# Mask factors in a room of the mixing from the first batch on, GpSimd for a pair's last sums, and another order of the last outputs, in a fused BigBird attention and Fourier mixing kernel

## The chip, the cores and the metric

The kernel runs on one core of a Trainium2 chip. A core has a matrix engine (TensorE, PE in the profile), VectorE (DVE), ScalarE (ACT), GpSimd (POOL), SyncE (SP), which here issues nearly all transfers, and 16 DMA engines that carry them. The metric is the device time of one execution in microseconds; the times shown are those of several runs, and the profile is that of one execution.

## The reference

Four batches of eight heads, 768 tokens, head width 64. Block-sparse attention with blocks of 32 tokens is followed by a Fourier mixing and a two-layer channel network on the 512 features of each token:

```python
scores = scale * q @ k.T
mask = near_diagonal | first_or_last_block | sampled_blocks      # by blocks of 32
attn = softmax(where(mask, scores, -1e9))
x = (attn @ v) laid out as (batch, token, head * width)

mixed = real(fft(fft(x, axis=1), axis=2))
u = x + mixed
un = (u - mean(u)) / sqrt(var(u) + 1e-6)
out = u + relu(un @ w_ch1) @ w_ch2          # w_ch1: 512 x 2048, w_ch2: 2048 x 512
```

The channel weights arrive as 64-bit floats, so they come as 16 MB and are rounded to 32 bits on the core.

## The kernel before

**Attention.** Two heads are a pair; there are 16 pairs, four to a batch. A pair has two halves of the queries (384 each) and six chunks of 128 keys, so 12 *units* (half, chunk), each a 128 x 768 tile of scores for both heads. Two units are a *slot*, 24 slots a batch. `scores` makes the score tiles on PE (line 570), `weigh` takes the exponent on ACT, `values` multiplies by v on PE (line 633) one slot later.

**The mask** is applied in two ways. In the first batch, and in the second until the channel network of batch 0 starts, PE adds a product of two small bf16 factors to the scores (`scores`, line 580), which puts blocked positions at a large negative value; such units are in `by_pe`, and ACT's exponent writes the weights directly (line 590). Later a 0/1 mask multiplies the exponents on DVE (lines 593 and 595). The factors are `of_k` and `off_q`; a third array, `keep_q`, serves to make the 0/1 mask. In the kernel before they lie in the two buffers of the pool `acc_p` (`at_k`, `at_q`). At slot 19 (`SB - 5`) `keep_factors` has GpSimd copy `of_k` and `off_q` to the large buffer `big2`, so that the `acc_p` buffers become free for batch 1.

**Row sums.** In batch 0 PE sums each unit's weights (`add_up`, line 701). From batch 1 on `gather` adds a half's six units up in a tile `acc` (pool `acc_p`, two buffers), either on DVE (line 614, one instruction of 128x768) or on GpSimd (line 619, two of 128x384), and `total` takes the sum over the partitions of both halves' `acc` on PE (line 715). For units in `by_pe`, `gather` is called in `values`, right after a unit's products, and picks the engine by the planner's clock; for the others it is called in `weigh`, and always GpSimd. The weights `e` have four buffers: the exponent of slot k+2 needs those of slot k released, by `values` and by `gather`.

**The channel weights.** 32 chunks of 512 KB come into large buffers `big0` to `big5` ("rooms", six of them, in turn: `w_load`), and `w_round` rounds each with two ACT instructions (lines 450, 453) and five on DVE (454 to 462), 1.42 chunks a slot. A chunk's load can go when the chunk six before it is rounded. `slot` emits the loads (`w_loads`) and then the rounding (`w_steps`). All loads stand in one queue on SP, in the order in which they are emitted: weights, q, k and v of coming pairs, and the cosine tables; one that must wait holds those behind it.

**The mixing** of batch b runs on PE, DVE and ACT between the slots of batch b+1, and that of the last batch after all attention. It folds x (`fold_0` to `fold_2`, DVE), multiplies by cosine and sine tables (`along`, `across`), normalizes (`spread`, `whiten`), transposes (`un_flip`), and then runs the channel network (`quad`, line 1032; `channels`, line 1088). The last batch uses `outputs` (line 1151), a form of block multiplication with seven products for each of three row tiles, twice; the results are added to the rows xA and xB on DVE (line 1158), and `store` sends finished rows out (line 1099).

**The order of the work** is written out by hand: instructions are emitted in program order for each engine. A planner keeps an estimated clock of each engine (`when`, advanced by `busy`), and places steps of the mixing (`gap`, `do_apart`) and short steps by those clocks; it also chooses DVE or GpSimd in `gather`. It runs when the program is built, not on the chip.

Of the kernel before, what the change touches and what calls it, by code (L numbers as in the profile page):

```python
# [11 lines left out]
FP32 = mybir.dt.float32  # L12
# [70 lines left out]
def _rows(view, tile):  # L83

    got = []
    for t, p0, runs, jump, n, s0, step in _ORDER:
        if t != tile:
            continue
        at = view[s0:s0 + 1, :]
        row, col = list(at.ap[0])[0], list(at.ap[1])  # L90
        if jump > 0:
            got.append((p0, runs * n, bass.AP(tensor=at.tensor, offset=at.offset,
                                              ap=[[jump * row, runs], [step * row, n], col])))
            continue
        for r in range(runs):
            at = view[s0 + r * jump:s0 + r * jump + 1, :]
            got.append((p0 + r * n, n, bass.AP(tensor=at.tensor, offset=at.offset,
                                               ap=[[step * row, n], col])))
    return got
# [3 lines left out]
def kernel(  # L103
# [14 lines left out]
    nc = tc.nc  # L118
# [73 lines left out]
    def busy(engine, us, after=0.0):  # L192
        when[engine] = max(when[engine], after) + us
        return when[engine]
# [10 lines left out]

    HOP = 0.1

    pairs = [(b, j) for b in range(B) for j in range(NP)]
    loaded, v_of = {}, {}

# [113 lines left out]
                                pattern=pat)  # L324


    at_k = acc_p.tile([P, 2, 2 * HS], BF16, tag="acc", name="at_k")
    at_q = acc_p.tile([P, 2, 2 * HS], BF16, tag="acc", name="at_q")
    of_k, off_q, keep_q = at_k[:, 0, :], at_q[:, 0, :], at_q[:, 1, :]

    nc.vector.memset(of_k, 0.0)
    nc.vector.memset(off_q, 0.0)
# [99 lines left out]
                              ap=[[2 * cols, P], [1, 2 * WN]])  # L432
                wchunks.append((src, w_sb[:, row, col:col + WN]))
    wraw = {}
    ROOMS = 6
    def room(i, shape, name, dtype=FP32):
        return big.tile(shape, dtype, tag=f"big{i}", name=name)

    def w_load(i):
        t = room(i % ROOMS, [P, 3 * WN], "wraw", U32)  # L440
        nc.sync.dma_start(out=t[:, 0:2 * WN].bitcast(I32), in_=wchunks[i][0])
        wraw[i] = t

# [25 lines left out]

    by_pe = set()
    factors = {"at": (of_k, off_q)}

    def keep_factors():

        kept = room(2, [P, 2, S], "factors", BF16)
        for a, t in enumerate(factors["at"]):
            nc.gpsimd.tensor_copy(out=kept[:, a, :], in_=t)
        factors["at"] = kept[:, 0, :], kept[:, 1, :]  # L480

    turned, e_of, acc_of, o_of, sums_of, x_of, sp_of = {}, {}, {}, {}, {}, {}, {}
    s_at, e_at, e_free, oT_at, acc_at = {}, {}, {}, {}, {}
# [69 lines left out]
    def scores(us):  # L553

        n, w = divmod(us[0], UP)
        half = w // C
        qT, kT = turned[n, 0], turned[n, 1]
        queries = slice(half * HS, (half + 1) * HS)
        got = []
        for u in us:  # L560
            c = u % C
            s = ps_s.tile([P, 2, 512], FP32, tag="s", name="s")
            got.append((u, s))
            if n < NP or (factors["at"] and True):
                by_pe.add(u)
            busy("PE", 0.72, max(e_at.get(u - SLOT, 0.0), z_at[u % 2]))
            s_at[u] = when["PE"] + HOP
            for i in range(2):
                rows = slice(D * i, D * i + D)
                nc.tensor.matmul(s[:, i, 0:HS], kT[rows, c * P:(c + 1) * P], qT[rows, queries],  # L570
                                 start=True, stop=u not in by_pe)
        for u, s in got:
            if u not in by_pe:
                continue
            c, (at_k, at_q) = u % C, factors["at"]
            busy("PE", 0.25)
            s_at[u] = when["PE"] + HOP
            for i in range(2):
                rows = slice(D * i, D * i + D)
                nc.tensor.matmul(s[:, i, 0:HS], at_k[rows, c * P:(c + 1) * P], at_q[rows, queries],  # L580
                                 start=False, stop=True)
        return got

    def weigh(u, s):
        n, w = divmod(u, UP)
        half, c = divmod(w, C)
        e = ep.tile([P, 2, HS], FP32, tag="e", name="e")
        e_of[u] = e
        if u in by_pe:
            nc.scalar.activation(out=e, in_=s[:, :, 0:HS], func=ACT.Exp, scale=scale)  # L590
            e_at[u] = busy("ACT", 0.8, max(s_at[u], e_free.pop(u - 2 * SLOT, 0.0))) + HOP
        else:
            nc.scalar.activation(out=s[:, :, 0:HS], in_=s[:, :, 0:HS], func=ACT.Exp, scale=scale)  # L593
            m = mask[:, c, half * HS:(half + 1) * HS].rearrange("p (o s) -> p o s", o=1)
            nc.vector.tensor_tensor(out=e, in0=s[:, :, 0:HS], in1=m.broadcast_to([P, 2, HS]),  # L595
                                    op=ALU.mult)
            e_at[u] = busy("DVE", 0.97, busy("ACT", 0.8, s_at[u]) + HOP) + HOP
            if n >= NP:
                gather(u)

    def gather(u):


        n, w = divmod(u, UP)
        half, c = divmod(w, C)
        if c == 0:
            return
        if c == 1:
            acc_of[n, half] = acc_p.tile([P, 2, HS], FP32, tag="acc", name="acc")
        acc, e = acc_of[n, half], e_of[u]  # L610
        start = e_of[u - 1] if c == 1 else acc
        at = max(e_at[u], acc_at.get((n, half), 0.0))
        if u in by_pe and factors["at"] and max(when["DVE"], at) + 1.0 < max(when["POOL"], at) + 2.9:
            nc.vector.tensor_tensor(out=acc, in0=start, in1=e, op=ALU.add)
            acc_at[n, half] = busy("DVE", 1.0, at) + HOP
        else:

            for i in range(2):
                nc.gpsimd.tensor_add(out=acc[:, i, :], in0=start[:, i, :], in1=e[:, i, :])  # L619
            acc_at[n, half] = busy("POOL", 2.9, at) + HOP  # L620
        e_free[u] = acc_at[n, half]

    def values(u):
        n, w = divmod(u, UP)
        half, c = divmod(w, C)
        e = e_of[u]
        busy("PE", 0.75, e_at[u])
        vt = v_of[n]
        if c == 0:
            o_of[n, half] = ps_o.tile([P, HS], FP32, tag="o", name="o")  # L630
        o = o_of[n, half]
        for i in range(2):
            nc.tensor.matmul(o[D * i:D * i + D, :], vt[:, i, c, :], e[:, i, :],  # L633
                             start=(c == 0), stop=(c == C - 1))
        if u in by_pe and n >= NP:
            gather(u)
        if c == C - 1:
            if half == 1:
                v_of.pop(n)
            oT = sum_p.tile([P, HS], FP32, tag="oT", name="oT")  # L640
            if in_blocks(n):
                nc.vector.transpose(out=oT, in_=o_of.pop((n, half)))
                oT_at[n, half] = busy("DVE", 0.5, when["PE"] + HOP) + HOP
            else:
                nc.scalar.copy(out=oT, in_=o_of.pop((n, half)))
                oT_at[n, half] = busy("ACT", 0.5, when["PE"] + HOP) + HOP
            o_of[n, half] = oT
# [295 lines left out]
    def mixer(b, xA, xB):  # L943
# [149 lines left out]
            if r == NF // 4 - 1:  # L1093
                store(half, m)

        def store(half, m):
            x = (xA, xB)[half]
            for p0, cnt, rows in _rows(out[b], T * half + m):
                nc.sync.dma_start(out=rows, in_=x[p0:p0 + cnt, m, :])
            if m == T - 1:  # L1100
                finished.add((b, half))

# [34 lines left out]
        def outputs(r, m, after):  # L1137
# [43 lines left out]
               in1=u.rearrange("p (o d) -> p o d", o=1).broadcast_to([P, 2, DH]), op=ALU.add)  # L1181
            busy("DVE", 0.7)
            plus(b1, p5)
            ahead(2)
            plus(b0, product(ps_s, "s", a22, rights[4]))
            if r == 1:
                store(1, m)
            ahead(3)
            p3 = product(ps_m, "m", o_s[m, 4], block(r, 1, 1))
            plus(a1, p3)  # L1190
            if r == 1:
                store(0, m)
            ahead(4)

        fl = [[("tm"[h == 1 and m != 1], lambda h=h, m=m: un_flip(h, m), 0.6, 0.55, 0.0)
               for m in range(T)]
# [105 lines left out]
    def begin(b):  # L1302


        before, after, rest = mixer(b, x_of[b, 0], x_of[b, 1])
        any_of = len(late) + len(apart) + 4 * len(rest)
        hold = 2 * T
        apart.extend((*step, any_of) for step in norm_steps(b) + before)
        apart.extend((*step, hold) for step in after)

        def go():
            late.extend(rest)
            factors["at"] = None
        apart.append(("-", go, 0.0, 0.0, 0.0, hold))

    def rest():
# [7 lines left out]
        return True  # L1324

    def w_loads():
        while state["got"] < min(len(wchunks), state["w"] + ROOMS):
            w_load(state["got"])
            state["got"] += 1

# [5 lines left out]
    def slot(sl):  # L1336
# [114 lines left out]
            item[2]()  # L1451
        w_loads()
        w_steps(sl)
        if sl == SB - 5:
            keep_factors()
        if sl >= 4 and sl % 2 == 0:
            table_step()

# [139 lines left out]
```

## Time and profile before

| | |
|---|---|
| median of 3 runs | 1077.72 us (1076.29 to 1078.42) |
| profiled execution | 1078.02 us, its span 1075.9 us |
| PE | 1042.7 us busy, 97% of the span |
| DVE | 665.4 us, 62% |
| ACT | 375.7 us, 35% |
| GpSimd | 231.1 us, 21% |
| mean granted PE clock | 0.991 |
| moved by DMA | 46.65 MB |

The span runs from the first to the last instruction of the core; the profiled execution takes 2.1 us more around it. Busy time is what the profile records for each engine; matmuls are pipelined, so busy is not the same as running at the peak. The granted clock is the share of full speed that PE was given. In the profile, lines with an L are lines of the kernel before, and a wait is put down to the engine and line that released it.

### The profile page before, as it was taken

How to read it: one execution, taken by the hardware profiler on the slowest of the kernel's cores; microseconds unless marked ns; L12 is line 12 of the kernel's file. 1: busy time of each engine (PE TensorE's matmuls, PEld its weight loads, DVE VectorE, ACT ScalarE, POOL GpSimd, SP SyncE). 2: the span in 40 equal slices, each digit the busy share in tenths (PEclk: the TensorE clock that was granted, in tenths of full speed). 3: DMA queues.
4: the chain of work that ended last, by engine and by line, in shares of the span. 5: the costliest groups of instructions: out<-in, count | busy, mean ns of one | idle time of the engine just before them, and what ended most of it. 6: DMA issues, size and time to landing. Idle time of an engine off the chain costs nothing.

```text
span 1075.9 us, 12388 instructions
## 1 busy us (share of the span) xinstructions
PE 1042.7 (97%) x4378; PEld 536.5 (50%) x4378; DVE 665.4 (62%) x1226; ACT 375.7 (35%) x742; POOL 231.1 (21%) x258
## 2 busy tenths in 40 slices
PE   8999898999999999999999999999999999999996
PEld 4433344444355555444444555443444555568575
DVE  5899694776771644664568446565556364675663
ACT  5998664563411202353352202243330302210210
POOL 1000080332700001256455001354630001000000
PEclk9999898999999999999999999999999999999998
DMA  7757230220100001222211000221000001000001
GB/s 225 222 176 240 58 71 15 45 45 16 29 1 1 0 1 30 59 38 42 54 27 33 0 1 10 69 40 31 15 8 8 0 1 30 30 1 1 1 18 44
DMA packets 120481, 46.65 MB, mean 43 GB/s; under 512 B 108110, under 2 KB 113244, under 8 KB 120412
## 3 DMA queue, kind: packets, MB, share of 16 engines
q1 hardware_dynamic: 118524, 44.99, 17.0%
q10 hardware_dynamic: 1856, 0.79, 0.3%
q8 instruction: 36, 0.59, 0.2%
q14 instruction: 33, 0.27, 0.1%
q0 software_dynamic: 32, 0.01, 0.0%
HBM read 37.11 MB, written 6.29 MB: 40 GB/s over the span
## 4 chain that ended last, share of the span: by engine, by line
PE 88%; DVE 7%; ACT 2%; issue 2%; POOL 1%; DMA 0%; ACTq 0%; DVEq 0%; POOLq 0%
PE y L1088 22%; PE z L1032 15%; PE s L570 12%; PE o L633 10%; PE yp L1032 7%; PE yy L1151 6%; PE xp L1032 4%; PE zp L842 2%; PE sp L701 1%; PE s L580 1%; PE zp L814 1%; PE utp L957 1%; DVE x L743 1%; PE sp L715 1%; PE tp L503 1%
## 5 line engine op out<-in xcount | busy, mean ns | idle before, releaser
L619 POOL TENSOR_TENSOR acc<-acc,e 128x384 f32<-128x384 f32 x150 | 152.1, 1050 | 85.3 <-DVE e L595 83.2
L570 PE MATMUL s<-qT,kT 64*128 64x384 f32 x768 | 154.4, 518 | 3.3 <-DVE e L595 1.9
L633 PE MATMUL o<-e,vr 128*64 128x384 f32 x768 | 142.8, 500 | 0.0
L1088 PE MATMUL y<-w_sb,hB 128*128 128x512 f32 x288 | 128.6, 596 | 1.4 <-DVE x L1091 1.4
L1088 PE MATMUL y<-w_sb,hA 128*128 128x512 f32 x288 | 129.2, 595 | 0.0
L1091 DVE TENSOR_TENSOR x<-y,x 128x512 f32<-128x512 f32 x72 | 49.7, 690 | 121.4 <-PE y L1088 121.2
L595 DVE TENSOR_TENSOR e<-s,mask 128x768 f32<-128x768 f32 x98 | 89.1, 950 | 56.8 <-ACT s L593 46.9
L593 ACT ACTIVATE s<-s 128x768 f32<-128x768 f32 x98 | 74.3, 792 | 93.3 <-PE s L570 93.0
L570 PEld LDWEIGHTS s<-qT,kT 64*128 64x128 f32 x768 | 64.3, 187 | 79.0 <-issue 24.1
L1032 PE MATMUL z<-unT,t 128*128 128x384 f32 x256 | 93.1, 486 | 0.7 <-DVE hA L1037 0.7
L590 ACT ACTIVATE e<-s 128x768 f32<-128x768 f32 x94 | 71.6, 814 | 47.7 <-PE s L580 33.9
L1088 PEld LDWEIGHTS y<-w_sb,hB 128*128 128x128 f32 x288 | 53.3, 190 | 67.3 <-issue 64.0
L905 POOL TENSOR_SCALAR st<-st 128x1 f32<-128x1 f32 x24 | 8.8, 365 | 355.2 <-DVE st L904 355.1
L1037 DVE TENSOR_TENSOR hA<-z,hA 128x384 f32<-128x384 f32 x64 | 35.7, 557 | 79.8 <-PE z L1032 79.8
L633 PEld LDWEIGHTS o<-e,vr 128*64 128x64 f32 x768 | 48.3, 137 | 71.6 <-issue 68.6
L1088 PEld LDWEIGHTS y<-w_sb,hA 128*128 128x128 f32 x288 | 53.1, 190 | 61.5 <-issue 58.4
L619 POOL TENSOR_TENSOR acc<-e 128x384 f32<-128x384 f32 x44 | 48.2, 1115 | 127.1 <-PE sp L715 93.6
L1041 ACT ACTIVATE hA<-hA 128x384 f32<-128x384 f32 x64 | 33.5, 523 | 119.0 <-DVE hA L1037 118.6
L1032 PEld LDWEIGHTS z<-unT,t 128*128 128x128 f32 x256 | 48.6, 190 | 35.0 <-DVE hA L1037 1.3
L1041 ACT ACTIVATE hB<-hB 128x384 f32<-128x384 f32 x64 | 33.5, 523 | 87.0 <-DVE hB L1037 87.0
L1052 ACT COPY hA<-xp 128x384 f32<-128x384 f32 x32 | 15.3, 478 | 107.0 <-PE xp L1032 107.0
L1032 PE MATMUL z<-t,w_sb 128*128 128x384 f32 x128 | 46.7, 488 | 0.9 <-DVE t L994 0.9
(206 smaller groups left out, 1439.2 us busy)
## 6 DMA issues: line engine op xcount, KB each, us to landing
wraw<-in_moe_w_ch_dram SPq DMA_DIRECT2D x32, 512.0 KB
vr<-in_v_dram SPq DMA_DIRECT2D x30, 192.0 KB
qb<-in_q_dram SPq DMA_DIRECT2D x44, 96.0 KB
kb<-in_k_dram SPq DMA_DIRECT2D x44, 96.0 KB
x<-oT SPq DMA_DIRECT2D x192, 12.0 KB
out_dram<-x SPq DMA_DIRECT2D x16, 128.0 KB
out_dram<-x SPq DMA_DIRECT2D x8, 256.0 KB
qr<-in_q_dram SPq DMA_DIRECT2D x24, 64.0 KB
```

The source lines that it names most:

```text
L570: nc.tensor.matmul(s[:, i, 0:HS], kT[rows, c * P:(c + 1) * P], qT[rows, queries], start=True, stop=u not in by_pe)
L590: nc.scalar.activation(out=e, in_=s[:, :, 0:HS], func=ACT.Exp, scale=scale)
L593: nc.scalar.activation(out=s[:, :, 0:HS], in_=s[:, :, 0:HS], func=ACT.Exp, scale=scale)
L595: nc.vector.tensor_tensor(out=e, in0=s[:, :, 0:HS], in1=m.broadcast_to([P, 2, HS]), op=ALU.mult)
L619: nc.gpsimd.tensor_add(out=acc[:, i, :], in0=start[:, i, :], in1=e[:, i, :])
L633: nc.tensor.matmul(o[D * i:D * i + D, :], vt[:, i, c, :], e[:, i, :], start=(c == 0), stop=(c == C - 1))
L1032: nc.tensor.matmul(to, a[:, k, :], c[:, k, :], start=(k == 0), stop=(k == ND // 2 - 1))
L1037: tt(out=to, in0=ps, in1=a, op=ALU.add)
L1041: nc.scalar.activation(out=h, in_=h, func=ACT.Relu)
L1088: nc.tensor.matmul(y, hs[0, half][:, l, m * P:(m + 1) * P], w2_sb[:, 4 * r + l, :], start=(l == 0), stop=(l == 3))
L1091: nc.vector.tensor_tensor(out=x[:, m, :], in0=y, in1=x[:, m, :], op=ALU.add)
L1151: nc.tensor.matmul(ps, a[:, k, :], c[k // 2][:, k % 2, :] if isinstance(c, list) else c[:, k, :], start=(k == 0), stop=(k == 3))
```

## The change

The three arrays `of_k`, `off_q` and `keep_q` lie in one tile in `big2` from the start. `keep_factors` and its two copies go. The weights use five rooms (0, 1, 3, 4, 5) in place of six, so a chunk's load waits for the chunk five before it and is emitted later in the program. Units in `by_pe` from batch 1 on are put in a list when they are weighed; they are gathered in `values` as before, but the last slot of a pair (its last two units) is gathered at once in `weigh`, after those that still stand in the list, and those two units always go to GpSimd. In `outputs` the product into xA's second half (`p3`) and its store come ahead of the product into xB's first half, whose store then comes last; for the very last tile xB's second half is stored as soon as it is done, and its first half in two pieces of 128 columns, one from SP's queue and one from ACT's.

```diff
+    def room(i, shape, name, dtype=FP32):
+        return big.tile(shape, dtype, tag=f"big{i}", name=name)
...
-    at_k = acc_p.tile([P, 2, 2 * HS], BF16, tag="acc", name="at_k")
-    at_q = acc_p.tile([P, 2, 2 * HS], BF16, tag="acc", name="at_q")
-    of_k, off_q, keep_q = at_k[:, 0, :], at_q[:, 0, :], at_q[:, 1, :]
+    factors = room(2, [P, 3, S], "factors", BF16)
+    of_k, off_q, keep_q = (factors[:, i, :] for i in range(3))
...
-    ROOMS = 6
+    W_ROOMS = (0, 1, 3, 4, 5)

     def w_load(i):
-        t = room(i % ROOMS, [P, 3 * WN], "wraw", U32)
+        t = room(W_ROOMS[i % len(W_ROOMS)], [P, 3 * WN], "wraw", U32)
...
-    by_pe = set()
-    factors = {"at": (of_k, off_q)}
-
-    def keep_factors():
-
-        kept = room(2, [P, 2, S], "factors", BF16)
-        for a, t in enumerate(factors["at"]):
-            nc.gpsimd.tensor_copy(out=kept[:, a, :], in_=t)
-        factors["at"] = kept[:, 0, :], kept[:, 1, :]
+    by_pe, to_gather = set(), deque()
+    masks = {"by_pe": True}
...
             e_at[u] = busy("ACT", 0.8, max(s_at[u], e_free.pop(u - 2 * SLOT, 0.0))) + HOP
+            if n >= NP:
+                to_gather.append(u)
+
+            if w >= UP - SLOT:
+                gather_to(u)
...
+    def gather_to(u):
+        while to_gather and to_gather[0] <= u:
+            gather(to_gather.popleft())
...
-        if u in by_pe and factors["at"] and max(when["DVE"], at) + 1.0 < max(when["POOL"], at) + 2.9:
+        if u in by_pe and masks["by_pe"] and w < UP - SLOT and max(when["DVE"], at) + 1.0 < max(when["POOL"], at) + 2.9:
...
-        if u in by_pe and n >= NP:
-            gather(u)
+        gather_to(u)
...
-        def store(half, m):
+        def store(half, m, cols=slice(0, DM), queue=nc.sync):
             x = (xA, xB)[half]
-            for p0, cnt, rows in _rows(out[b], T * half + m):
-                nc.sync.dma_start(out=rows, in_=x[p0:p0 + cnt, m, :])
+            for p0, cnt, rows in _rows(out[b][:, cols], T * half + m):
+                queue.dma_start(out=rows, in_=x[p0:p0 + cnt, m, cols])
...
             plus(b1, p5)
+            ends = r == 1 and after is None
+            if ends:
+                store(1, m, slice(DH, DM))
             ahead(2)
-            plus(b0, product(ps_s, "s", a22, rights[4]))
-            if r == 1:
-                store(1, m)
-            ahead(3)
             p3 = product(ps_m, "m", o_s[m, 4], block(r, 1, 1))
             plus(a1, p3)
             if r == 1:
                 store(0, m)
+            ahead(3)
             ahead(4)
+            plus(b0, product(ps_s, "s", a22, rights[4]))
+            if ends:
+                store(1, m, slice(0, P))
+                store(1, m, slice(P, DH), nc.scalar)
+            elif r == 1:
+                store(1, m)
...
-        while state["got"] < min(len(wchunks), state["w"] + ROOMS):
+        while state["got"] < min(len(wchunks), state["w"] + len(W_ROOMS)):
...
-        if sl == SB - 5:
-            keep_factors()
```

The lines left out replace `factors["at"]` by `masks["by_pe"]` where it served as a flag, and by `of_k` and `off_q` where the mask product is made.

More of the change, by code (lines that the diff above doesn't have):

```diff
@@ L434 @@
     wraw = {}
-    ROOMS = 6
-    def room(i, shape, name, dtype=FP32):
-        return big.tile(shape, dtype, tag=f"big{i}", name=name)
+    W_ROOMS = (0, 1, 3, 4, 5)
     def w_load(i):
-        t = room(i % ROOMS, [P, 3 * WN], "wraw", U32)
+        t = room(W_ROOMS[i % len(W_ROOMS)], [P, 3 * WN], "wraw", U32)
         nc.sync.dma_start(out=t[:, 0:2 * WN].bitcast(I32), in_=wchunks[i][0])
@@ L563, in scores @@
             got.append((u, s))
-            if n < NP or (factors["at"] and True):
+            if n < NP or masks["by_pe"]:
                 by_pe.add(u)
@@ L574, in scores @@
                 continue
-            c, (at_k, at_q) = u % C, factors["at"]
+            c = u % C
             busy("PE", 0.25)
@@ L579, in scores @@
                 rows = slice(D * i, D * i + D)
-                nc.tensor.matmul(s[:, i, 0:HS], at_k[rows, c * P:(c + 1) * P], at_q[rows, queries],
+                nc.tensor.matmul(s[:, i, 0:HS], of_k[rows, c * P:(c + 1) * P], off_q[rows, queries],
                                  start=False, stop=True)
@@ L634, in values @@
                              start=(c == 0), stop=(c == C - 1))
-        if u in by_pe and n >= NP:
-            gather(u)
+        gather_to(u)
         if c == C - 1:
@@ L1312, in go @@
             late.extend(rest)
-            factors["at"] = None
+            masks["by_pe"] = False
         apart.append(("-", go, 0.0, 0.0, 0.0, hold))
```

## The prediction

> **What bounds the kernel now.** I read the page first.
>
> ```profile
> PE 1042.7 (97%) x4378; PEld 536.5 (50%) x4378; DVE 665.4 (62%) x1226; ACT 375.7 (35%) x742; POOL 231.1 (21%) x258
> PEclk9999898999999999999999999999999999999998
> ```
>
> PE is the bound: only what lets it start earlier, idle less or run at full clock can move the time. PE ends at 1066.9 and sits idle 24.2 us before that, 2.6 of it at the start. The clock row has two dips, in the fifth and seventh slice. The list of waits shows what lies there.
>
> ```profile
> POOL factors L479 <- DVE w_sb L462: 105.6, 1, 105.6
> PE s L580 <- POOL factors L479: 6.1, 1, 6.1
> PE sp L715 <- DVE acc L614: 3.8, 1, 3.8
> ```
>
> They are the two longest waits of PE. The timeline gives their places.
>
> ```profile
> 109.86 0.69 DVE L462 TENSOR_TENSOR w_sb<-w_sb,wraw 128x512 f32<-128x512 f32 x1
> 110.68 0.82 POOL L479 COPY factors<-at_k 128x768 bf16<-128x768 bf16 x1 [105.58 <-DVE w_sb L462]
> 112.33 0.82 PE L580 MATMUL s<-factors 64*128 64x384 bf16 x4 [6.15 <-POOL factors L479]
> 150.38 10.24 POOL L619 TENSOR_TENSOR acc<-acc,e 128x384 f32<-128x384 f32 x6 [0.16 <-ACT e L590]
> 165.01 0.95 DVE L614 TENSOR_TENSOR acc<-acc,e 128x768 f32<-128x768 f32 x1
> 166.01 1.50 PE L715 MATMUL sp<-acc,pick 128*32 128x384 f32 x4 [3.84 <-DVE acc L614]
> ```
>
> Stall 1: the mask product of slot 20 waits for the copied factors, the copy for room 2, and that for chunk 26, on which DVE works until 110.55. Stall 2: the total of the first pair of batch 1 waits for one last addition, which stands on DVE behind the folds of batch 0. The windows of the clock show what each costs beyond its idle time.
>
> ```profile
> 103.30:110.10 6.80, 2.88 (x22) 1.21 (x20) 6.53 (x17) 2.20 (x9) 0.00 (x0) 1.00 0.71 217
> 110.10:116.90 6.80, 4.58 (x20) 1.20 (x20) 0.45 (x1) 1.51 (x2) 1.59 (x2) 0.50 0.37 121
> 157.90:164.70 6.80, 4.27 (x26) 1.39 (x24) 6.73 (x8) 2.75 (x5) 4.99 (x4) 1.00 0.35 83
> 164.70:171.60 6.90, 5.59 (x17) 2.19 (x18) 5.47 (x10) 1.60 (x3) 0.00 (x0) 0.51 0.01 2
> 226.20:233.00 6.80, 5.09 (x34) 2.10 (x32) 5.39 (x9) 3.55 (x10) 1.47 (x3) 1.00 0.01 1
> ```
>
> Columns: stretch, length, busy of PE, weight loads, DVE, ACT, GpSimd, then clock. A stretch with 3.9 or 2.5 us of PE idle is followed by one at half clock; the last, with 1.7 us idle, was not (no dip in its slice).
>
> [...]an addition on GpSimd takes 1.0 us at the median, and 1.7 each (10.24 for six) beside the folds.[...]
>
> **The change, part by part** (against the profiled execution: span 1075.9, 1078.0 in all; the median, 1077.7, is 1.8 above the span).
>
> *Factors stay where they are.* The copies go (two of 0.82 us on GpSimd, which was idle), and with them stall 1. Slot 20's scores start at 104.6 and slot 21's at 117.5, 12.9 us. Their PE work is scores 1.5, mask 0.4, values 1.5, sums 0.85 and the end of a transpose 0.35, 4.6 us. Gain 12.9 - 4.6 = 8.3: 6.15 of idle and 2.2 from half clock. What is late next? DVE's rounding, which itself stood still from 110.55 to 120.09 for ACT, and ACT for PE; it gains 9.5, so it keeps pace, and PE's lead over it is as before.
>
> *Five rooms for six.* Every load from chunk 5 on is emitted one chunk later, so some go a slot later in SP's queue, behind what waits there.
>
> ```profile
> 51.92 0.33 SPq L441 DMA_DIRECT2D wraw<-in_moe_w_ch_dram  x1
> 60.82 1.15 SPq L372 DMA_DIRECT2D tab<-in_cos_s_dram  x2
> 62.06 3.85 SPq L253 DMA_DIRECT2D qr<-in_q_dram  x6
> 66.02 1.49 SPq L441 DMA_DIRECT2D wraw<-in_moe_w_ch_dram  x3
> ```
>
> The first row is chunk 15. It moves from slot 8 to slot 9: behind the table load that SP holds until 60.82 (DVE must free its buffer) and behind q, so to 66.0. A load issued there landed at 70.1 by the completion records, and ACT wants it at 68.23.
>
> ```profile
> 68.23 0.68 ACT L450 ACTIVATE wraw<-wraw 128x512 f32<-128x512 uint32 x1
> 69.38 1.49 ACT L590 ACTIVATE e<-s 128x768 f32<-128x768 f32 x2
> 71.12 1.56 PE L570 MATMUL s<-qT,kT 64*128 64x384 f32 x8
> ```
>
> ACT is late by 1.9, the exponents behind it too. The first of them ends at 70.2 now and at 72.1 then, while PE wants its bank at 71.12: PE loses 1.0. In the same way I walked through the other chunks: 21, 22 and 24 come 1 to 1.7 us after ACT's present time for them, but by then PE is 1.0 late and the exponent has 0.6 to 2 us of cover, so about 0.1 in all; the rest land 0.3 to 10 us early. Cost +1.1; bounds 0 (the loads also start earlier) and +3 (no cover at all at chunks 15, 21 and 24).
>
> *GpSimd takes the last two units.* In the first pair of batch 1, GpSimd already adds units 8, 9 and 10 (the six instructions to 160.62) and DVE unit 11, at 165.01. Now unit 11 follows on GpSimd: two instructions of 1.0 to 1.3 us (2.27 for the next two), so acc is whole at about 163.0, and PE, which comes to it at 162.17, waits 0.9 in place of 3.84. If the planner gives unit 8 or 9 to DVE, whose clock is behind at that earlier place, GpSimd is done near 159 and the wait is gone. Then no stretch has over 1.7 us idle and the clock stays whole: of 166.0 to 171.6, 5.6 us at half clock, 2.8 come back. Gain 2.9 + 2.8 = 5.7; bounds 1 (the wait only shortens and the clock is halved all the same) and 6.6. Behind that addition stand the next pair's sums on GpSimd, and ACT's second exponent, which waited 4.59 for the same DVE addition: released earlier too. In the three later pairs of batch 1, GpSimd idles from 164.6 to 194.3 and has 4 us for two units well within the two slots until the weights' buffer is wanted: nothing. The planner's clocks shift and may move mixing steps by a place: 0, bounds -1.5 (the 1.99 us idle at 231.3, ACT's order, goes) and +1.5.
>
> *Order of the last outputs.* Each product still ends 1.73 us after the one before and DVE has 0.3 to 1.3 us idle between, so PE's end doesn't move. After it the stores count.
>
> ```profile
> 1072.00:1073.00 1.00, 0.00 (x0) 0.00 (x0) 0.00 (x0) 0.00 (x0) 0.00 (x0) 0.50 0.13 49
> 1073.00:1074.00 1.00, 0.00 (x0) 0.00 (x0) 0.00 (x0) 0.00 (x0) 0.00 (x0) 0.50 0.12 47
> ```
>
> A DMA share of 0.12 is two engines of 16. They carry xB's last tile, issued at 1065.68 as 2 x 64 rows: 256 KB at 48 GB/s is 5.4 us, and it lands at 1073.66; the stores of xA, 64 rows each, spread over 16 and queue behind it on those two, to 1074.4. In the new form all three pieces of xB still have the outer size 2[...]. So these two still carry 256 KB, in smaller packets (a packet of 2048 bytes takes 84 ns, of 1028 bytes 47, so 12% slower), from 0.54 us earlier: end at -0.5 + 0.6 = +0.1. I take 0; bounds -1.5 (ACT's pieces go on two other engines) and +0.7.
>
> **Sum:** -8.3 + 1.1 - 5.7 + 0 + 0 = -12.9. Span 1063.0, median 1077.7 - 12.9 = **1064.8**.
>
> **The rivals.** *A, the forecast*: both stalls go, small price for the room; 1062 to 1067.5; 0.62. *B: the second wait only changes its owner.* GpSimd is slowed by the folds (1.7 us an instruction), two units queue, PE idles over 2.5 us near the total and the clock is halved again. For it: 10.24 us for six; against: unit 10 is already in those. 8.3 + 1 - 1.1 = 8.2 gained, 1069.5; 0.20. *C: more than that*: full 6.6, nothing lost on the rooms, a shorter tail: 17 gained, 1060.5; 0.09. *D, slower: the rooms starve ACT.* 27 loads move. If each were late as chunk 15 is, PE would lose 1.0 on each, 27 us, and stretches with over 2.5 us idle would add 3.4 at half clock. It decides once 14 of the 27 cost that (8.3 + 5.7 = 14.0); at 20 the time is 1084. Against it: by the list above most land early, and waits of ACT for weights are none now; 0.07. *E: no change*, if stall 1 were DVE's and not the copy's, so that another wait holds PE until 112: the waits name nothing else there; 0.02.
>
> The range takes in A, B and half of C: low end 8.3 + 6.6 + 1.5 + 1 = 17.4 gained, 1060.3; high end 8.3 + 1 - 3 - 0.7 = 5.6, 1072. Within 0.2% (2.2 us) a measurement of this kernel can't be told from no change, its three runs spreading 2.1. Faster 0.91, same 0.02, slower 0.07.
>
> **What would show it.** No copy at L479, no wait of L580 on GpSimd, slot 21 some 4.6 us after slot 20; waits of ACT L450 for DMA, near chunk 15, and PE idle of about 1 us there; no clock dip in the fifth and seventh slice; the total's wait on POOL and below 1 us; 7 us from the last DVE addition to the last landing, as before, with two engines busy. It is wrong if PE idles again in 106 to 112, if a dip returns at the total, or if weights' waits add up to more than 3 us on PE.

## The result, and the profile after

The changed kernel takes 1064.96 us (median of 4 runs, 1064.72 to 1065.31); the kernel before took 1077.95 in the 4 runs beside it. The ratio is 0.9882, with an interval of 0.9865 to 0.9900: 13.0 us less, where 12.9 had been forecast. The profiled execution has a span of 1063.0 us and a mean granted clock of 0.997. The sum was right, but two of its terms were not, and by luck they nearly cancel.

The page of the kernel after, its first part and the clock row of its second:

```profile
PE 1036.9 (98%) x4390; PEld 535.2 (50%) x4390; DVE 654.1 (62%) x1217; ACT 375.3 (35%) x742; POOL 235.9 (22%) x262
...
PEclk9999999999999999999999999999999999999998
```

Both dips of the clock row are gone. PE is idle for 14.8 us before its end in place of 24.2, and the longest idle stretch after the start is 1.3 us. PE's last matmul ends at 1051.76, 15.2 us earlier than before. The span is only 12.9 us shorter: 2.2 us have been lost behind PE's end.

The place of the first long wait is not on the list of waits any more. Slot 20 starts at 105.5 us and slot 21 at 109.9, 4.4 us apart; in the kernel before they stood 12.9 us apart. At the place of the second, the timeline of the kernel after shows this (start and length in us; the brackets hold the idle time before, and who ended it):

```profile
146.83 0.95 DVE L617 TENSOR_TENSOR acc<-acc,e 128x768 f32<-128x768 f32 x1
...
147.92 6.16 POOL L622 TENSOR_TENSOR acc<-acc,e 128x384 f32<-128x384 f32 x4 [2.63 <-DVE acc L617]
...
153.55 1.42 PE L717 MATMUL sp<-acc,pick 128*32 128x384 f32 x8
```

The last three units of the pair are unit 9 on DVE, then units 10 and 11 on GpSimd, four instructions that end at 154.1. The total needs them only for its last matmuls and starts without a wait. Before, GpSimd had units 8, 9 and 10 and DVE unit 11, behind the folds. So the planner did not only move the last unit: at the earlier place in the program, where DVE's estimated clock was behind, it gave unit 9 to DVE.

The first of the moved loads, chunk 15, shows in three timelines of the kernel after: SP's queue, ACT and PE.

```profile
65.20 1.49 SPq L441 DMA_DIRECT2D wraw<-in_moe_w_ch_dram  x3
```

```profile
67.06 0.47 ACT L365 CAST mask<-m 128x384 uint8<-128x384 f32 x1
69.44 0.70 ACT L450 ACTIVATE wraw<-wraw 128x512 f32<-128x512 uint32 x1 [1.91 <-DVE w_sb L462]
```

```profile
71.43 1.62 PE L563 MATMUL s<-qT,kT 64*128 64x384 f32 x8 [1.06 <-ACT e L583]
```

ACT is 1.91 us late and PE loses 1.06, as worked out (1.9 and 1.0). The releaser named on ACT's line is DVE, which was long done: what came last was the load, which landed at 69.36. One more load comes late, chunk 21, which landed at 88.72 (ACT's timeline, then PE's):

```profile
88.80 0.71 ACT L450 ACTIVATE wraw<-wraw 128x512 f32<-128x512 uint32 x1 [1.25 <-DMA wraw<-in_moe_w_ch_dram]
```

```profile
90.84 1.61 PE L563 MATMUL s<-qT,kT 64*128 64x384 f32 x8 [0.42 <-ACT e L583]
```

Last, the end of the span, a window for each microsecond (stretch, length, busy of PE, weight loads, DVE, ACT, GpSimd; clock, DMA share, GB/s):

```profile
1055.00:1056.00 1.00, 0.00 (x0) 0.00 (x0) 0.00 (x0) 0.00 (x0) 0.00 (x0) 1.00 0.14 10
1056.00:1057.00 1.00, 0.00 (x0) 0.00 (x0) 0.00 (x0) 0.00 (x0) 0.00 (x0) 0.90 0.12 34
1057.00:1058.00 1.00, 0.00 (x0) 0.00 (x0) 0.00 (x0) 0.00 (x0) 0.00 (x0) 0.50 0.16 52
1058.00:1059.00 1.00, 0.00 (x0) 0.00 (x0) 0.00 (x0) 0.00 (x0) 0.00 (x0) 0.50 0.14 44
1059.00:1060.00 1.00, 0.00 (x0) 0.00 (x0) 0.00 (x0) 0.00 (x0) 0.00 (x0) 0.50 0.11 35
```

A DMA share of 0.11 to 0.16, about two engines of 16, carries the rest, as before (0.12 and 0.13), but for longer and mostly at a lower rate (34 to 52 GB/s, before 47 and 49), and in one of these microseconds almost nothing moves (10 GB/s). By the completion records the last store lands 9.2 us after PE's end (1060.95); before, it was 7.5 us. From the last landing to the end of the span it is 2.05 us; before, 1.50.

Put side by side by the starts of the slots, after less before, the 12.9 us of the span are:

| stretch | us |
|---|---|
| start (the clock opens at 5.5 us after the first instruction, before at 7.7) | -0.8 |
| chunk 15 (1.1) and chunk 21 (0.5) | +1.6 |
| slot 20 to 21, the first long wait | -8.5 |
| the second long wait, and what follows it in batch 1 | -7.5 |
| behind PE's end | +2.2 |

The first row I take for chance: over the runs of this study the clock opened between 5.4 and 8.7 us (from there on a warm-up product takes 275 ns in place of 421), and the kernel before and its version with the sums alone, which begin alike, opened at 7.7 and 5.45. In the kernel after the first scores start at 8.17 us, before at 8.98: 0.8 for 2.2 of clock.

### The profile page after: what moved, and what is told of

Read it like the earlier page. It is cut to its first block, busy times and chain, and to the rows that moved or that the text cites. A ratio compares the mean times of both kernels' runs of the same rounds, so it can differ in the third digit from the quotient of the medians.

```text
span 1063.0 us, 12409 instructions
## 1 busy us (share of the span) xinstructions
PE 1036.9 (98%) x4390; PEld 535.2 (50%) x4390; DVE 654.1 (62%) x1217; ACT 375.3 (35%) x742; POOL 235.9 (22%) x262
## 4 chain that ended last, share of the span: by engine, by line
PE 88%; DVE 4%; DMA 3%; ACT 2%; issue 1%; SPq 1%; POOL 0%; ACTq 0%; DVEq 0%
PE y L1090 23%; PE z L1034 15%; PE s L563 12%; PE o L636 10%; PE yp L1034 7%; PE yy L1153 7%; PE xp L1034 4%; PE zp L844 2%; PE s L573 1%; DMA out_dram<-x 1%; PE zp L816 1%; DMA wraw<-in_moe_w_ch_dram 1%; PE sp L717 1%; PE utp L959 1%; PE sp L703 1%
## 5 line engine op out<-in xcount | busy, mean ns | idle before, releaser
L622 POOL TENSOR_TENSOR acc<-acc,e 128x384 f32<-128x384 f32 x158 | 159.6, 1047 | 93.8 <-DVE e L593 75.1
L593 DVE TENSOR_TENSOR e<-s,mask 128x768 f32<-128x768 f32 x92 | 84.0, 951 | 57.9 <-ACT s L591 47.9
L591 ACT ACTIVATE s<-s 128x768 f32<-128x768 f32 x92 | 69.9, 792 | 87.7 <-PE s L563 87.3
L583 ACT ACTIVATE e<-s 128x768 f32<-128x768 f32 x100 | 76.3, 820 | 33.9 <-PE s L573 28.6
L1034 PE MATMUL xp<-unT,w_sb 128*128 128x384 f32 x128 | 47.2, 492 | 0.0
```

The costliest lines, as they stand in the source:

```text
L1034: nc.tensor.matmul(to, a[:, k, :], c[:, k, :], start=(k == 0), stop=(k == ND // 2 - 1))
```

## The experiments

All comparisons are with the kernel before, 1077.6 to 1078.0 us beside them.

**The parts one by one.** First, the kernel before with only the factors and the five rooms:

```diff
-    at_k = acc_p.tile([P, 2, 2 * HS], BF16, tag="acc", name="at_k")
-    at_q = acc_p.tile([P, 2, 2 * HS], BF16, tag="acc", name="at_q")
...
+    fixed = room(2, [P, 3, S], "factors", BF16)
...
-    ROOMS = 6
+    W_ROOMS = (0, 1, 3, 4, 5)
...
-        if sl == SB - 5:
-            keep_factors()
```

> The kernel before with the factors in room 2 from the start and five rooms for the weights; sums and outputs as before. The prediction's step: stall 1 goes (8.3 us) and the rooms cost 1.1 to 1.6, so about 1071 against 1078, one clock dip left (at the total), PE idle 3.8 there. Rival: the second stall is only a consequence of the first (DVE late with the rounding), and goes with it: 1065, no dip. Rival: DVE's rounding was what held PE, and another wait takes the place of the copy: 1077 or more.

Measured: 1071.04 us (1069.97 to 1071.63), ratio 0.9937 (0.9921 to 0.9954), 6.9 us less than before; -8.3 + 1.1 = -7.2 was forecast for these two steps. The first long wait is gone and the other stands as it was. Its line in PE's timeline of this run:

```profile
159.61 1.49 PE L708 MATMUL sp<-acc,pick 128*32 128x384 f32 x4 [3.84 <-DVE acc L607]
```

Second, the kernel before with only the new place and engine of the sums:

```diff
+            if n >= NP:
+                to_gather.append(u)
+            if w >= UP - SLOT:
+                gather_to(u)
...
-        if u in by_pe and factors["at"] and max(when["DVE"], at) + 1.0 < max(when["POOL"], at) + 2.9:
+        if u in by_pe and factors["at"] and w < UP - SLOT and max(when["DVE"], at) + 1.0 < max(when["POOL"], at) + 2.9:
...
-        if u in by_pe and n >= NP:
-            gather(u)
+        gather_to(u)
```

> The kernel before with only the sums changed (last two units of a pair gathered when weighed, on GpSimd). The prediction's step: the wait of the total shortens or goes and the clock stays whole there: 5.7 to 6.6 us, about 1071.5 to 1072.3, stall 1 and its dip unchanged. Rival: GpSimd beside the folds is as late as DVE was, PE idles over 2.5 us there and the clock is halved all the same: 1077.

Measured: 1069.15 us (1068.44 to 1069.69), ratio 0.9925 (0.9908 to 0.9941), 8.8 us less. That is 2 to 3 us more than forecast. In its trace the wait at the total and the half clock behind it are gone (3.84 + 2.8 = 6.6), and so are the idle stretches of 1.99 us at 231.3 and 1.02 at 288.5 of the kernel before; 1.15, 1.28 and 0.74 have come at other places. In this profiled execution the span is 9.3 us shorter: 1.2 of it is an early start, which is chance, 0.5 lies at the first wait, and 7.6 behind it, where the edit works. The first wait stands (6.19 us).

Third, only the order of the outputs:

```diff
+            if ends:
+                store(1, m, slice(DH, DM))
...
-            plus(b0, product(ps_s, "s", a22, rights[4]))
...
+            plus(b0, product(ps_s, "s", a22, rights[4]))
+            if ends:
+                store(1, m, slice(0, P))
+                store(1, m, slice(P, DH), nc.scalar)
```

> The kernel before with only the outputs changed (order, pieces, two queues). The prediction's step: nothing (1078, between -1.5 and +0.7). What the profile after suggests: PE's end doesn't move, but from there to the end of the span it takes 11.2 in place of 9.0 us: slower by 2.2, 1080.

Measured: 1079.2 us (1077.68 to 1083.17, 20 runs), ratio 1.0013 (1.0006 to 1.0019): slower, by 1.3 to 1.4. From the other side, the kernel after with the old order of the outputs:

```diff
-            ends = r == 1 and after is None
-            if ends:
-                store(1, m, slice(DH, DM))
             ahead(2)
+            plus(b0, product(ps_s, "s", a22, rights[4]))
+            if r == 1:
+                store(1, m)
+            ahead(3)
             p3 = product(ps_m, "m", o_s[m, 4], block(r, 1, 1))
...
-            plus(b0, product(ps_s, "s", a22, rights[4]))
-            if ends:
-                store(1, m, slice(0, P))
-                store(1, m, slice(P, DH), nc.scalar)
```

> The changed kernel with the outputs of before. If the new outputs cost 2.2 us: 1062.8, faster than the changed kernel's 1065.0. If they cost nothing, as predicted: 1065.0.

Measured: 1063.1 us (1062.54 to 1063.34), ratio 0.9865 (0.9849 to 0.9882). The span ends 9.0 us after PE, in place of 11.2. The new order and its pieces cost about 1.9 us, where I had put 0.

**What the end depends on.** If the two engines are the limit, what counts is how early their bytes are issued and in what packets. So in the kernel after I wrote the last tile's products in an order that finishes xB after five of the seven, sends it in one store, and leaves for the end xA, whose 64-row stores spread wider (while they ran in the kernel after, from 1053 to 1054 us, the DMA share was 0.93):

```diff
+            if r == 1 and after is None:
+                plus(u, product(ps_t, "t", a21, rights[2]), u)
+                plus(a1, u)
+                plus(u, product(ps_s, "s", o_s[m, 3], rights[3]), u)
+                p5 = product(ps_o, "o", o_s[m, 1], rights[1])
...
+                plus(b1, p5)
+                plus(b0, product(ps_s, "s", a22, rights[4]))
+                store(1, m)
+                plus(a1, p5)
+                plus(a0, product(ps_m, "m", a12, block(r, 1, 0)))
+                plus(a1, product(ps_m, "m", o_s[m, 4], block(r, 1, 1)))
+                store(0, m)
+                return
```

> The changed kernel; in the very last tile the products are ordered so that both halves of xB are done after five of the seven, stored in one transfer, and xA comes last. If the end is set by xB's 256 KB on two engines: issued 3.0 us ahead of PE's end, landed some 7.9 later, the xA stores behind it on those two: end of the span 7 us after PE's in place of 11.2, so about 1060.8 against 1065.0. If the end is set by the last store, whatever it is: as with the outputs of before, 1063.

Measured: 1060.85 us (1060.11 to 1062.39), ratio 0.9844 (0.9828 to 0.9861). The span ends 7.2 us after PE; 7.0 had been worked out. Its last windows, in the same columns:

```profile
1054.00:1055.00 1.00, 0.00 (x0) 0.00 (x0) 0.00 (x0) 0.00 (x0) 0.00 (x0) 1.00 0.87 221
1055.00:1056.00 1.00, 0.00 (x0) 0.00 (x0) 0.00 (x0) 0.00 (x0) 0.00 (x0) 1.00 0.33 107
1056.00:1057.00 1.00, 0.00 (x0) 0.00 (x0) 0.00 (x0) 0.00 (x0) 0.00 (x0) 0.93 0.13 49
1057.00:1058.00 1.00, 0.00 (x0) 0.00 (x0) 0.00 (x0) 0.00 (x0) 0.00 (x0) 0.50 0.02 8
```

Only one microsecond remains in which two engines work alone (a share of 0.13); in the kernel after there are five (0.11 to 0.16).

Do two queues help? The kernel after with the second of the last pieces from GpSimd's queue, and then with both on SP's:

```diff
-                store(1, m, slice(P, DH), nc.scalar)
+                store(1, m, slice(P, DH), nc.gpsimd)
```

> The changed kernel; the very last piece of 128 columns goes from GpSimd's queue in place of ACT's. If the cost is that both last pieces share two engines, and GpSimd's queue takes two others[...]: 1.5 to 2.5 us less, about 1063. If the price is small packets or memory, wherever they go: 1065.[...]

Measured: 1062.91 us (1062.36 to 1063.6), ratio 0.9861 (0.9845 to 0.9878): 2.0 less than after, as "two other engines" would have it. The end is 8.7 us behind PE. But nothing in the packets of this trace speaks for other engines. GpSimd's piece goes in 16 packets of 4096 bytes, not in 128 of 512, in two series of eight. These start at 1057.440 and 1057.835, each 5 to 6 ns after the start of the packet that ends one of the two series of SP's piece (1057.434 and 1057.830). The records name no engine; so close a succession, twice, would fit the same two, which is my reading and is not shown. Of the 2.5 us that the end gains in the trace, 1.2 come from xA's last packets, which are done 3.8 us after PE's end in place of 5.1, for which the traces give no reason; 0.5 lie behind the last landing, of which more below. So the time hit the forecast, and the mechanism that went with it was not seen.

```diff
-                store(1, m, slice(P, DH), nc.scalar)
+                store(1, m, slice(P, DH))
```

> The changed kernel with both last pieces from SP's queue. If two engines carry both anyway, ACT's queue buys nothing: 1065.0 within 0.5. If the second queue hides an issue that would count, it is slower by that, 0.6: 1065.6.

Measured: 1064.78 us (1063.53 to 1065.62), ratio 0.9874 (0.9857 to 0.9890): the same as after. In the profiled execution the end is 10.3 us behind PE, in place of 11.2, so ACT's queue won nothing and may have cost up to 1 us. The trace of the kernel after shows the two pieces side by side: from 1057.7 on, packets of SP's piece and of ACT's take turns in the same two series, one start every 23.5 ns in each. What decides which engines a transfer gets, no run here shows.

**Place or engine.** The change to the sums has two edits: the last two units are added earlier in the program, and always on GpSimd. The kernel after with the early place, but the engine chosen by the planner's clock:

```diff
-        if u in by_pe and masks["by_pe"] and w < UP - SLOT and max(when["DVE"], at) + 1.0 < max(when["POOL"], at) + 2.9:
+        if u in by_pe and masks["by_pe"] and max(when["DVE"], at) + 1.0 < max(when["POOL"], at) + 2.9:
```

> The kernel after, but the engine of a pair's last two units is chosen by the planner's clock as for the others (the condition that keeps them on GpSimd is gone); they are still added early, right behind their exponents. Theory 'it is the engine': one of the two goes to DVE behind the folds of batch 0 again, PE waits some 3 to 4 us for the total with a half-clock stretch behind it, 1068 to 1071. Theory 'it is the early place': an addition that stands earlier in DVE's order comes ahead of the folds, no wait at the total, 1065 as after.

Measured: 1071.03 us (1069.96 to 1073.71), ratio 0.9942 (0.9925 to 0.9959). That is 6.1 more than after (in the profiled executions 6.6, of it 1.2 at the start of the clock). The size is that of "it is the engine", but the wait is another one. Its timeline:

```profile
149.06 2.02 DVE L617 TENSOR_TENSOR acc<-acc,e 128x768 f32<-128x768 f32 x2
...
151.47 0.85 PE L717 MATMUL sp<-acc,pick 128*32 128x384 f32 x8
...
157.56 0.55 DVE L685 COPY sums<-sp 128x384 f32<-128x384 f32 x1
...
158.17 0.55 PE L659 MATMUL xt<-ident,oT 128*128 128x128 f32 x3 [2.59 <-DVE sums L685]
```

DVE takes both units, ahead of the rest of the folds. The total is ready at 151.47, earlier than anywhere else. But then the copy of the total (L685) stands behind the folds until 158.1, PE's next transpose wants that PSUM bank, and PE waits 2.59 us for it; a stretch at half clock follows.

And the other half: GpSimd, but at the old place, one slot later:

```diff
-            if w >= UP - SLOT:
-                gather_to(u)
```

> The kernel after, but the last two units of a pair are added where the others are, behind their products with v one slot later; GpSimd still takes them. Theory 'it is the engine': GpSimd's own order is the same, so 1065 as after, to within 0.7. Theory 'it is the early place': the wait at the total is back in part, 1067 to 1070.

Measured: 1068.5 us (1068.09 to 1069.05), ratio 0.9915 (0.9897 to 0.9932), 3.5 more than after (in the profiled executions 4.3, of it 0.9 at the start of the clock). The place counts too. Its timeline:

```profile
143.98 12.54 POOL L620 TENSOR_TENSOR acc<-acc,e 128x384 f32<-128x384 f32 x8
...
156.56 0.81 ACT L583 ACTIVATE e<-s 128x768 f32<-128x768 f32 x1 [1.28 <-POOL acc L620]
...
157.27 0.47 ACT L658 COPY x<-xt 128x384 f32<-128x384 f32 x1
...
157.89 1.25 PE L715 MATMUL sp<-acc,pick 128*32 128x384 f32 x8 [2.19 <-ACT x L658]
```

Here all of units 8 to 11 go to GpSimd (at the later place the planner chose it for unit 9 too), 1.57 us an instruction beside the folds, and it ends at 156.52. An exponent of ACT waits for the weights' buffer that GpSimd still reads, the copy of x stands behind that exponent, and the total waits for the bank that this copy frees. Half clock follows here too, for 3.4 us.

**What a wait of PE costs.** To measure it by itself I put a chain of 25 copies of one column on DVE and a transpose on PE that waits for the last into the kernel after, in a stretch where PE is never idle (the probe takes no part in the computation):

```diff
+            if (b, r, half, m) == (1, 2, 0, 1):
+                probe = sm.tile([P, 1], FP32, tag="nm", name="probe")
+                nc.vector.tensor_copy(out=probe, in_=y[:, 0:1])
+                for _ in range(24):
+                    nc.vector.tensor_copy(out=probe, in_=probe)
+                row = ps_t.tile([1, P], FP32, tag="t", name="probe_row")
+                nc.tensor.transpose(row, probe, ident)
```

> The kernel after with a probe in the channel network of batch 1, where PE is never idle: 25 copies of one column on DVE, each on the one before, then a transpose on PE that waits for the last. The chain takes some 2.5 to 4 us; it is not part of the computation and leaves the output as it is. Theory 'a wait costs its idle time alone': total longer by what PE is idle there and no more. Theory 'a wait of over about 2.5 us is followed by one window at half clock': idle time plus up to 3.4 us, so 4 + 3.4 = some 7.4 us, 1072; with an idle of only 2 us or less no halving, 1067.

Measured: 1073.89 us (1073.11 to 1074.52), ratio 0.9961 (0.9947 to 0.9975), 8.9 more than after. In the profiled executions it is 8.7; 1.6 of that lies ahead of the probe, 1.2 at the start of the clock. The chain took longer than I had thought, 4.64 us (186 ns a copy), and PE idled 5.47. By the starts of PE's products ahead of and behind it, the probe cost 7.1. The windows are cut at the edges of its half-clock stretch, in steps of 3.41 us:

```profile
612.82:616.23 3.41, 1.99 (x5) 0.57 (x3) 2.60 (x12) 0.00 (x0) 0.00 (x0) 1.00 0.00 0
616.23:619.64 3.41, 0.00 (x0) 0.00 (x0) 2.79 (x19) 0.00 (x0) 0.00 (x0) 1.00 0.01 2
619.64:623.06 3.42, 2.78 (x5) 1.26 (x6) 1.20 (x5) 0.00 (x0) 0.79 (x2) 0.50 0.00 0
623.06:626.47 3.41, 3.41 (x17) 2.21 (x16) 0.69 (x1) 0.00 (x0) 0.00 (x0) 1.00 0.00 0
```

An empty window is followed by one at half clock. PE was busy for 2.78 us of that one, so by my estimate half of that, 1.4 us, was lost on top of the idle time, and 5.47 + 1.4 = 6.9 of the 7.1 are told. It is a wait with a tax, but a smaller tax than the 3.4 at most that I had expected. That figure was too high from the start: one window of 3.41 us at half clock can't cost more than half of it, 1.7.

**The rooms, and the best of all.** The kernel after with each slot's loads emitted behind the rounding that frees their room, so that chunk 15 goes in its old slot:

```diff
+        w_steps(sl)
         w_loads()
-        w_steps(sl)
```

> The changed kernel with each slot's weight loads emitted behind its rounding, so that chunk 15 stands ahead of the table load in SP's queue again, with five rooms. If the price of the fifth room is the late chunk: PE's 1.06 us before the scores of slot 13 and the 0.4 near chunk 24 go, 1063.5. If it is the room itself: 1065.

Measured: 1064.06 us (1062.91 to 1064.64), ratio 0.9870 (0.9853 to 0.9886). PE's idle stretches of 1.06 us at 70.4 (chunk 15) and 0.42 near 90 (chunk 21, not 24) are gone, and PE ends at 1050.33, 1.4 earlier; in that execution 0.5 of it was lost again at the end of the span. The gain in the medians is 0.9, close to the range of the runs, so its sign rests on the trace more than on the time. With the order that ends xB first on top, so two edits that are both shown above:

```diff
+            if r == 1 and after is None:
...
+                plus(b0, product(ps_s, "s", a22, rights[4]))
+                store(1, m)
...
+        w_steps(sl)
         w_loads()
-        w_steps(sl)
```

> The kernel after with two changes at once: the last row tile's products in the order that ends xB after five of seven and stores it in one piece, and in every slot the loads of the weights behind the rounding that frees their room. If the two gains add up (4.1 and 0.9 us in their own runs) 1059.9; if the loads' gain is none beside the other, 1060.9.

Measured: 1059.59 us (1058.9 to 1059.9), ratio 0.9832 (0.9814 to 0.9849). The two gains add up within the spread of the runs (4.1 and 0.9 apart, 5.4 together). This version is 5.4 us faster than the kernel after and 18.0 faster than the kernel before.

## Why the prediction was right, and where it was not

**The factors: right.** -8.3 was forecast for the first wait, of it 2.2 from half clock; the slots show -8.5. DVE's rounding was not late next, as argued: no wait of PE came in its place.

**Five rooms: right in kind, slightly small.** Chunk 15 cost 1.06 (1.0 forecast). The rest was put at 0.1 and cost 0.5, at chunk 21, where I had counted on cover. Together 1.6 in the trace, and with the factors -6.9 in the time against -7.2.

**GpSimd for the last units: the sign right, the size and the way not.** The base case of this step was that unit 11 follows unit 10 on GpSimd, acc is whole 0.9 us after PE wants it, and the clock stays whole. The run with GpSimd at the late place is that case, and there PE waited 2.19 us and the clock was halved. GpSimd's end was as forecast, 0.8 us after PE went idle (156.52 against 155.70), but it was not what came last: I had named ACT's exponent as released earlier, but not that a copy stands behind it on ACT, whose bank the total needs. What happened in the change was the clause that I had put beside it, that the planner gives unit 8 or 9 to DVE; that took the wait away. The forecast of 5.7 became about 7.5, since all 6.6 at the total came back and PE's other idle stretches behind it are 1.0 us shorter in sum (those of 1.99 and 1.02 went; 1.31, 1.15 and 0.74 came), which I had put into the bounds of the planner's shift only. Neither edit alone did it: the early place without GpSimd moves the wait to the copy of the total, GpSimd without the early place to ACT. What no run separates is the early place from the engine of unit 9, which the planner gave to DVE at the early place and to GpSimd at the late one.

**The order of the last outputs: wrong.** The step said that the two engines carry the same 256 KB in smaller packets from 0.54 us earlier, so -0.5 + 0.6 = +0.1. That ACT's piece goes with SP's on the same two was an assumption; in the trace their packets take turns in the same two series (one start every 23.5 ns in each). The step measured +1.4 and +1.9 in the times, +2.2 in the trace. The start and the packets were sized rightly. What was put at nothing, without a reason, is what failed: that the two engines carry an unbroken stream, and that behind the last packet all stays as it was.

- The start, -0.57: the first packet of xB starts 0.61 us ahead of PE's end; before, 0.04.
- The packets, +0.6: on one engine, packets of 2048, 1024 and 512 bytes start 80, 42 and 23.5 ns behind one another. So 64 of 2048 are 5.1 us, and 64 of 1024 with 128 of 512, as the pieces went, are 5.7.
- The stream, +1.3: the two engines needed 9.0 us from the first packet of xB to the last of all, for an estimated 6.4 us of packets (those 5.7, and eight of 2048 bytes of xA on each); before, 7.1 for 5.8. Much of it lies behind the landing of the first piece, at 1054.87: packets of xA, most often of 84 ns, took up to 907 there, and the last pieces, issued from 1052.24 on, start only behind them, at 1056.39 and 1056.82 on the two engines. Why these packets were slow the traces don't tell. The old stream had a loss too, which the prediction missed: from its first packet (1066.88) to its landing (1073.66) 6.8 us passed, not 5.4.
- Behind the last packet, +0.9: it took 0.8 us to land in place of 0.4, and from there to the end of the span it is 2.05 us in place of 1.50. For the second part the traces have a reason. SP checks the stores' semaphores one after another, eight in 0.55 us (1060.97 to 1061.52). ACT's piece, which lands last (1060.95), is the first on its list, and seven others follow; in the kernel before, what landed last (1074.42) was the last on the list (1074.44). With both pieces from SP's queue the last landing is the second on the list, and the end comes 1.96 us behind it; with GpSimd's piece, which isn't on SP's list, 1.51. The other runs fit: 2.05 or 2.06 with ACT's piece, 1.50 or 1.51 where the old store or xA lands last.

That an early xB is the cure was shown: 7.2 us from PE's end to that of the span.

**The sum.** -8.3 + 1.1 - 5.7 + 0 against -8.5 + 1.6 - 7.5 + 2.2, and -0.8 of chance. The total agreed to 0.1 us by luck, because 1.8 more at the sums, 0.8 at the start and 0.2 at the factors paid for 2.2 at the end and 0.5 at the rooms. Rival B, a second wait that only changes its owner, did not happen here, but it is what both halves of the edit do alone, at 1071.0 and 1068.5; it had been put at 1069.5. Rival D, starving ACT, fell: ACT waited for weights at two places only, 1.9 and 1.2 us. Rival C's 17 us was more than its own parts give, 8.3 + 6.6 + 1.5 = 16.4; nothing rests on it.

## What to carry to other kernels

Here an idle stretch of PE was worth its length plus the half clock behind it, where there was one: behind those of 2.19 to 6.19 us there was, behind those of 1.3 us and less in the kernel after there was none, and of two of 2.0 us one had it. So first take away the long ones. When an operation is moved to another engine, follow what stands behind it on both engines, up to the buffers that these free: here each half of one edit only moved the wait, and the two together removed it. At the end of a kernel, count the bytes on each DMA engine, and let what is confined to few engines be issued first: here xB's 256 KB went over two of 16, and the order that sends them first was 4.1 us faster. A second queue was not seen here to bring a second set of engines: look in the packets whether it brought any, even when the time comes out as if it had.

## What the runs showed of the hardware

The half-clock stretches, between the start and PE's end, took 3.4 or 6.8 us. It was 6.83 in both places in the kernel before, and 6.8 with the factors alone (at the total) and with the sums alone (at the first wait). It was 3.4 in both runs with one half of the sums' edit, in the probe's, and at one place in the run of the outputs alone. There PE had idled for 2.00 us ahead of a transpose; ahead of the same transpose the kernel before idled for 1.99, and no half clock followed. Windows of 3.41 us, cut in steps from the half-clock stretches of each run, first of the kernel before:

```profile
229.59:233.00 3.41, 1.70 (x12) 0.69 (x8) 3.17 (x7) 3.28 (x9) 1.29 (x2) 1.00 0.01 2
233.00:236.41 3.41, 3.13 (x21) 1.82 (x23) 1.36 (x2) 1.60 (x4) 0.27 (x1) 1.00 0.72 115
```

and of the kernel before with the outputs alone:

```profile
230.57:233.99 3.42, 1.53 (x10) 0.56 (x6) 3.28 (x6) 3.29 (x9) 1.48 (x2) 1.00 0.01 2
233.99:237.40 3.41, 3.30 (x11) 1.83 (x13) 1.17 (x2) 0.53 (x2) 0.07 (x1) 0.50 0.57 92
```

With 1.70 us of PE busy in a window the clock stayed, with 1.53 it was halved in the next one. Of the idle stretch, 1.71 us lie in the first window and 0.28 in the next in the one run, 1.89 and 0.11 in the other. The windows just ahead of the other half-clock stretches held less of PE: 0.00 and 0.86 us in the kernel before, 0.28 with the factors alone, 0.82 with the early place by the clock, 1.22 with GpSimd at the late place, 0.00 in the probe's run, where the window before that held 1.99 and the clock stayed. What decides, the traces don't show.

The ends of the stretches, in the same windows: with the factors alone a window at half clock with 2.71 us of PE busy was followed by a second, and so were those with 1.23 and 2.13 in the kernel before; in the probe's run one with 2.78 was the last, in the run of the outputs alone one with 3.30. The start of a run is slow too. PE begins at 2.6 us, and a warm-up product takes 421 ns and starts 213 ns behind the one before it. From 5.5 us on in the kernel after, and from 7.7 in the kernel before, it is 275 and 111 ns; in the run of the sums alone the clock opened at 5.45, in the run with one queue at 8.74. The traces show no reason for these differences.
